# Top-k attention with two MLPs on one Trainium2 core: the hand-over to the first MLP block gets priority, score evictions go by whole tiles, rounding goes to GpSimd, and two weight rows start early

## The chip, the cores and the metric

The kernel runs on 1 core of one Trainium2 chip (trn2). The metric is device time in microseconds (us); the time before is the median of 3 runs. The engines are TensorE (PE in the profile, its weight loads PEld), VectorE (DVE), ScalarE (ACT), GpSimd (POOL) and SyncE (SP, which issues the loads and stores). Each engine works its own queue strictly in the order in which the program was built.

## The reference

Attention for 4 batches and 8 heads, 576 tokens, head dimension 64, in which each row of scores keeps its 32 largest; then two MLPs over the 2304 tokens of 512 values. q, k and v are float32; the weights reach the kernel as float64.

```python
scores = scale * np.matmul(q, k.transpose(0, 1, 3, 2))
kth = np.partition(scores, -top_k, axis=-1)[..., -top_k:-top_k + 1]
scores = np.where(scores >= kth, scores, -1000000000.0)
attn = np.exp(scores - np.max(scores, axis=-1, keepdims=True))
attn = attn / (np.sum(attn, axis=-1, keepdims=True) + 1e-09)
x = np.matmul(attn, v)                    # to (2304, 512)
h = np.maximum(x @ w_in, 0.0);   x = h * h @ w_out           # first MLP, d_ff 2048
h = x @ w_in2;   out = np.maximum(0.01 * h, h) @ w_out2      # second MLP
```

## The kernel before, in words

**High and low parts.** To keep float32 accuracy at the fast matmul format, most operands are split in two: a rounded high part and the low part left over (`xh`, `xl`; weights `wi`, `wo` hold both; so do `KT` and `q`). The high part is a rounding copy (`split_hi`, on ScalarE for the units in `HI_SET` and on GpSimd otherwise), the low part a subtraction, mostly on GpSimd. A product of two split operands takes three matmuls.

**Attention.** The tokens are cut into 9 units of 64 to 320 tokens (`UNITS`), each for 4 head pairs; these give 144 tiles of 128 rows, which are worked in 72 pairs. For a tile, TensorE makes scores in two halves of 288 columns (`scores`), ScalarE copies each half out of PSUM, VectorE finds the 32 largest by four MAX8 and three MATCH_REPLACE8 passes, ScalarE makes the exponentials (`drop`, `expo_sum`) with a shift `nb` from GpSimd (`shifts`), the sum's reciprocal `rc` takes a step on GpSimd and one on VectorE (`recip`), TensorE transposes (`pt_main`, `pt_left`) and multiplies with v (`av`), and `x_out` writes `xh` (ScalarE) and `xl` (GpSimd) for that head pair's 128 rows of x. Batches 2 and 3 (`EARLY`) have their scores made ahead of time: tiles `sp` in PSUM, copied into `stage` and stored to DRAM (`sd`), loaded again later. This filling runs over the slots `FILL`. Batch 0 uses PSUM tiles `sd`, batch 1 `att`. PSUM has 8 banks: 3 for `att`, and before the MLPs begin `SPB` for `sp` and `SDB` for `sd`.

**MLPs.** The tokens form 6 blocks (`BLOCKS`, the first of 512). A phase is one block and one MLP: 16 weight rows f, each with 12 matmuls into `h` (4 head pairs c, three products), the activation (ScalarE, GpSimd), and 12 matmuls that add into 4 `acc` banks. In the first two phases the weight rows are fresh: each is loaded (`wraw`), passed through two ScalarE passes and two VectorE steps (these make float32 out of the float64 words), rounded on ScalarE, subtracted on GpSimd, and stored (`wd`) for later phases.

**What sets the order.** Everything is put at slots; a slot is about one VectorE pass, 16 to a pair (`at`). A scheduling layer then makes each engine's queue out of this, by priorities: steps put at slots have a raised one, the MLPs' matmuls none. Block 0 needs units 0 and 1, that is pairs 0 to 15; it begins when `x_out` of pair 15's head pair has been put down.

Of the kernel before, what the change touches and what calls it, by code (L numbers as in the profile page):

```python
# [71 lines left out]
def topk_attention_moe_moe2_kernel(  # L72
# [117 lines left out]


# [361 lines left out]
    def moe(j, layer):  # L553
# [5 lines left out]
        gs = {}  # L559
        for f in range(NF + LAG):  # L560
            conv = iter(())
            if f < NF:
# [5 lines left out]
                h = late["psum"].tile([P, 512], F, tag="h", name="h", bufs=1)  # L568
                cnt = 0
                if f == 0:  # L570
                    mm = [(w, c, 0) for w in range(2) for c in range(NK)] + [(0, c, 1) for c in range(NK)]
                else:
                    mm = [(0, c, y) for c in range(NK) for y in range(2)] + [(1, c, 0) for c in range(NK)]
                for w, c, y in mm:
                    PE.matmul(h[:, 0:n], lhsT=wi[:, w, c * P:(c + 1) * P], rhs=x[c][y][:, 0:n], start=cnt == 0,  # L575
                              stop=cnt == 3 * NK - 1)
                    cnt += 1
                    if cnt % MQ == 0 and cnt < 3 * NK:
# [326 lines left out]
```

## Time and profile before

| | |
|---|---|
| median of 3 runs | 1211.68 us (1209.5 to 1212.38) |
| the profiled execution's own time | 1210.15 us |
| its span, first to last instruction | 1208.4 us, 20261 instructions |
| busy in the span | PE 94%, PEld 82%, DVE 78%, ACT 67%, POOL 57% |
| mean granted TensorE clock | 0.98 of full |

The shares are means over stages that differ: VectorE is nearly full until about 970 us and has little to do behind that, while the MLPs go on to the end on TensorE. The time of a run is a little longer than the span, by what lies ahead of the first and behind the last instruction.

### The profile page before, as it was taken

The numbers are of one execution on the slowest core, as the hardware profiler recorded it, in microseconds if no ns is written. First come the engines' busy times: TensorE is split into PE (matmuls) and PEld (weight loads), VectorE is DVE, ScalarE is ACT, GpSimd is POOL, SyncE is SP. The second block draws the span as 40 slices with busy tenths as digits, with TensorE's granted clock in tenths as the row PEclk, the third lists the DMA queues.
The fourth block names the chain that finished last, engine by engine and source line by source line (L and its number), as shares of the span: only waits on it lengthen the run. The fifth ranks groups of instructions, "written<-read, shape, count | busy, mean of one in ns | idle before, by whom it ended". The sixth has DMA issues, their size and how long they took to land.

```text
span 1208.4 us, 20261 instructions
## 1 busy us (share of the span) xinstructions
PE 1135.8 (94%) x6388; PEld 992.5 (82%) x6388; DVE 946.5 (78%) x1944; ACT 807.5 (67%) x1831; POOL 682.8 (57%) x982
## 2 busy tenths in 40 slices
PE   4988987999889999999999999999999999999998
PEld 3776765887678779988999898888788899999997
DVE  7999899868988999999999999999999930110122
ACT  6988898878998986766656666555666653334322
POOL 7765564877878876556666665555565644004300
PEclk9899897999999999999999999999999999999999
DMA  9765566779989888879988888776676679779974
GB/s 307 255 217 192 192 220 222 267 233 333 342 280 319 305 267 263 296 269 384 355 293 290 298 272 286 221 227 226 201 239 211 199 255 369 253 253 341 356 256 135
DMA packets 110522, 323.25 MB, mean 268 GB/s; under 512 B 17488, under 2 KB 25680, under 8 KB 110416
## 3 DMA queue, kind: packets, MB, share of 16 engines
q1 hardware_dynamic: 107776, 317.24, 77.5%
q10 hardware_dynamic: 2640, 4.72, 1.1%
q8 instruction: 52, 0.85, 0.3%
q14 instruction: 54, 0.44, 0.1%
HBM read 254.54 MB, written 67.37 MB: 266 GB/s over the span
## 4 chain that ended last, share of the span: by engine, by line
PE 71%; ACT 11%; DVE 7%; DMA 6%; issue 2%; POOL 1%; ACTq 0%; SPq 0%; POOLq 0%; DVEq 0%
PE h L575 29%; PE acc L620 14%; PE acc L618 14%; PE att L408 4%; PE att L313 4%; DVE m L829 3%; PE att L397 3%; DVE w L831 3%; DMA wraw<-in_w_dram 2%; DMA sd<-stage 2%; ACT stage L277 1%; ACT e L299 1%; ACT e L295 1%; ACT s L277 1%; PE sp L276 1%
## 5 line engine op out<-in xcount | busy, mean ns | idle before, releaser
L575 PE MATMUL h<-xh,wi 128*128 128x512 f32 (+2 forms) x1280 | 349.9, 345 | 13.4 <-ACT gb L597 4.2
L829 DVE MAX8 m<-w 128x8 f32<-128x576 f32 x432 | 311.9, 748 | 1.1
L575 PEld LDWEIGHTS h<-xh,wi 128*128 128x128 f32 x1280 | 227.5, 191 | 42.6 <-ACT gb L597 5.8
L831 DVE MATCH_REPLACE8 w<-m,w 128x576 f32<-128x576 f32 x288 | 213.5, 744 | 0.8
L575 PE MATMUL h<-xl,wi 128*128 128x512 f32 (+2 forms) x640 | 207.6, 342 | 0.6 <-DVE xl L632 0.6
L601 POOL TENSOR_TENSOR gl<-ga,gh 128x512 fp32r<-128x512 f32 (+2 forms) x160 | 162.7, 1017 | 37.9 <-ACT gh L600 32.1
L618 PE MATMUL acc<-gh,wo 128*128 128x512 f32 (+2 forms) x768 | 156.8, 340 | 0.0
L620 PE MATMUL acc<-wo,gh 128*128 128x512 f32 x576 | 152.5, 399 | 2.9 <-ACT gh L600 2.7
L598 POOL TENSOR_TENSOR ga<-ga,gb 128x512 f32<-128x512 f32 (+2 forms) x80 | 81.4, 1017 | 130.6 <-ACT gb L597 127.3
L618 PEld LDWEIGHTS acc<-gh,wo 128*128 128x128 f32 x768 | 126.5, 189 | 11.0 <-ACT gh L586 0.2
L575 PEld LDWEIGHTS h<-xl,wi 128*128 128x128 f32 x640 | 121.4, 191 | 12.3 <-DVE xl L632 1.1
L295 ACT ACTIVATE e<-s,m 128x576 f32<-128x576 f32 x144 | 111.7, 779 | 18.6 <-DVE m L829 13.4
L620 PEld LDWEIGHTS acc<-wo,gh 128*128 128x128 f32 x576 | 104.3, 189 | 24.1 <-ACT gh L600 5.0
L829 DVE MAX8 m<-s 128x8 f32<-128x576 f32 x144 | 104.1, 748 | 12.5 <-ACT s L277 6.1
L299 ACT ACTIVATE e<-e,nb 128x576 f32<-128x576 f32 x144 | 111.0, 774 | 3.2 <-POOL nb L289 2.8
L587 POOL TENSOR_TENSOR ga<-ga 128x512 f32<-128x512 f32 (+2 forms) x80 | 66.1, 827 | 78.1 <-ACT gh L586 72.8
L831 DVE MATCH_REPLACE8 w<-m,s 128x576 f32<-128x576 f32 x144 | 107.1, 744 | 0.6
L313 PE MATMUL att<-ident,e 128*128 128x128 f32 x576 | 90.8, 281 | 13.7 <-ACT e L299 5.1
L313 PEld LDWEIGHTS att<-ident,e 128*128 128x128 f32 x576 | 70.0, 143 | 27.4 <-ACT e L299 10.1
L308 POOL TENSOR_SCALAR e<-e,rc 128x576 f32<-128x576 f32 x108 | 79.8, 749 | 22.5 <-DVE rc L304 21.1
L585 ACT ACTIVATE ga<-h 128x512 f32<-128x512 f32 (+2 forms) x80 | 39.0, 488 | 77.4 <-PE h L575 71.9
L618 PE MATMUL acc<-gl,wo 128*128 128x512 f32 (+2 forms) x384 | 87.7, 345 | 0.1
(94 smaller groups left out, 2136.7 us busy)
## 6 DMA issues: line engine op xcount, KB each, us to landing
wi<-wd SPq DMA_DIRECT2D x160, 512.0 KB, 5.0
wo<-wd SPq DMA_DIRECT2D x160, 512.0 KB, 5.2
wraw<-in_w_dram SPq DMA_DIRECT2D x64, 512.0 KB, 6.0
sd<-stage SPq DMA_DIRECT2D x72, 288.0 KB, 2.9
s<-sd SPq DMA_DIRECT2D x72, 288.0 KB, 4.6
wd<-wi SPq DMA_DIRECT2D x32, 512.0 KB, 5.4
wd<-wo SPq DMA_DIRECT2D x32, 512.0 KB, 5.9
kraw<-in_k_dram SPq DMA_DIRECT2D x16, 576.0 KB, 5.4
```

The lines of the kernel that those rows point to most:

```text
L295: ACT.activation(t["e"], t["s"], AF.Prelu, bias=pr["m8"][:, i, 31:32], scale=-1.0, alpha=0.125 / FAR)
L299: ACT.activation(e, e, AF.Exp, bias=pr["nb"][:, i:i + 1], scale=-FAR, accum_out=pr["sum"][:, i:i + 1])
L308: POOL.tensor_scalar(e, e, pr["rc"][:, i:i + 1], 1.0, op0=OP.mult, op1=OP.mult)
L313: PE.transpose(ps[:, j * P:(j + 1) * P], t["e"][:, j * P:(j + 1) * P], ident)
L575: PE.matmul(h[:, 0:n], lhsT=wi[:, w, c * P:(c + 1) * P], rhs=x[c][y][:, 0:n], start=cnt == 0, stop=cnt == 3 * NK - 1)
L587: POOL.tensor_tensor(a[:, 0:n], a[:, 0:n], a[:, 0:n], op=OP.mult)
L598: POOL.tensor_tensor(a[:, 0:n], a[:, 0:n], b[:, 0:n], op=OP.subtract)
L601: (DVE if j >= GLD else POOL).tensor_tensor(gl[:, 0:n], a[:, 0:n], gh.bitcast(F)[:, 0:n], op=OP.subtract)
L618: PE.matmul(acc[c][:, 0:n], lhsT=wo[:, w, cs], rhs=g[:, 0:n], start=first, stop=last)
L620: PE.matmul(acc[c], lhsT=g[:, cs], rhs=wo[:, w, :], start=first, stop=last)
L829: cur["dve"] = DVE.max(out=m8[:, x, 8 * r:8 * r + 8], in_=t["s"] if r == 0 else t["w"])
L831: cur["dve"] = DVE.match_replace(out=t["w"], in_to_replace=m8[:, x, 8 * r:8 * r + 8], in_values=t["s"] if r == 0 else t["w"], imm_value=NEG)
```

## The change

- `scores`: for the batches made ahead, both halves go to one two-bank PSUM tile and are copied out by one 576-column copy. `SPB` is 2 of these (4 banks), `SDB` 1.
- `FILL` ends at slot 215 in place of 245.
- `HI_SET` is (0, 1): from the third head pair of unit 0 on, the rounding of q, k and v goes from ScalarE to GpSimd.
- Pair 15 (`first_done`): its steps from `shifts` to `x_out` are put right behind its last MAX8 and with a higher priority (`urgent`); its `av` goes in two halves by head, the first earlier.
- Weight rows 0 and 1: their ScalarE passes are made early (`lead_passes`, into PSUM banks of `sp`), their VectorE steps and the rounding, now on GpSimd, are put at pair 15's end (`lead_bits`).
- In the first phase, weight rows 0 and 1 have the 9 products of the first three head pairs issued ahead (`AHEAD`); the last head pair's three follow when it is there. Row 1 uses an `acc` bank for it. `ga` has 3 buffers.

```diff
@@ constants
-FILL = (2, 245)
+FILL = (2, 215)
-SDB = 2
-SPB = 3
+SDB = 1
+SPB = 2
+URGENT = 800
-HI_SET = (0, 1, 2, 3, 4, 5, 6, 7, 8, 9, 10, 11, 12, 13, 14, 15)
+HI_SET = (0, 1)
@@ scores
-            ps = stage_psum.tile([P, 512], F, tag="sp", name="sp", bufs=SPB)
+            if half == 0:
+                t["ps"] = stage_psum.tile([P, 2, 512], F, tag="sp", name="sp", bufs=SPB)
+            ps = t["ps"][:, half]
...
-        ACT.activation(t["s"][:, ks], ps[:, 0:HALF], AF.Copy)
+        if direct(uh):
+            ACT.activation(t["s"][:, ks], ps[:, 0:HALF], AF.Copy)
+        elif half == 1:
+            ACT.activation(t["s"].rearrange("p (x c) -> p x c", x=2), t.pop("ps")[:, :, 0:HALF], AF.Copy)
@@ new
+    def urgent(fn):
+        def run(*a):
+            with tc.high_priority(offset=URGENT):
+                fn(*a)
+        return run
...
+    def lead_passes(i):
+        led[i] = []
+        for raw, w in zip(wraw.pop(i), w_alloc(i)):
+            lo, hi = raw[:, :, 0], raw[:, :, 1]
+            b = pool.tile([P, 512], U, tag="wc", name="wc", bufs=WCB)
+            if not led[i]:
+                vs = stage_psum.tile([P, 2, 512], F, tag="sp", name="sp", bufs=SPB)
+            v = vs[:, len(led[i])]
+            ACT.activation(b, lo, AF.Copy, scale=L_SCALE, bias=L_BIAS)
+            ACT.activation(v, hi.bitcast(F), AF.Copy, scale=H_SCALE)
+            led[i].append((b, v.bitcast(U), w))
+
+    def lead_bits(i):
+        for b, vu, w in led.pop(i):
+            with behind("dve"):
+                DVE.scalar_tensor_tensor(b, vu, 3, b, op0=OP.logical_shift_left, op1=OP.bitwise_or)
+            DVE.scalar_tensor_tensor(b, vu, 0x80000000, b, op0=OP.bitwise_and, op1=OP.bitwise_or)
+            split_hi(w[:, 0, :], b.bitcast(F))
+            POOL.tensor_tensor(w[:, 1, :], b.bitcast(F), w.bitcast(F)[:, 0, :], op=OP.subtract)
@@ moe
+        ahead_of = AHEAD if j == 0 and layer == 0 else 0
+        for f in range(ahead_of):
+            hs[f] = late["psum"].tile([P, 512], F, tag="acc" if f else "h", name="h", bufs=4 if f else 1)
+            mm = [(w, c, y) for c in range(NK - 1) for w, y in ((0, 0), (1, 0), (0, 1))]
+            for i, (w, c, y) in enumerate(mm):
+                PE.matmul(hs[f][:, 0:n], lhsT=wt[base + f][0][:, w, c * P:(c + 1) * P], rhs=x[c][y][:, 0:n],
+                          start=i == 0, stop=False)
...
+                if f in hs:
+                    h = hs.pop(f)
+                    mm = [(w, NK - 1, y) for w, y in ((0, 0), (1, 0), (0, 1))]
...
-                a = late["mlp"].tile([P, 512], F, tag="ga", name="ga", bufs=2)
+                a = late["mlp"].tile([P, 512], F, tag="ga", name="ga", bufs=3)
@@ pairs and av
+        if p == first_done:
...
+            at(z + 13, urgent(shifts), pr)
+            for i in range(2):
+                at(z + 13, urgent(drop), pr, i)
+                at(z + 13, urgent(expo_sum), pr, i)
+            at(z + 13, urgent(recip), pr)
+            for i in range(2):
+                at(z + 14, urgent(pt_main), pr["t"][i])
+            at(z + 14, urgent(pt_left), pr)
+            continue
...
-        apart = uh["n"] > P and uh["n"] % P and uh["ti"] % 2 == 0
+        tight = uh["last"] // 2 == first_done
+        apart = uh["n"] > P and (uh["n"] % P or tight) and uh["ti"] % 2 == 0
...
+                at(z + i, urgent(av) if near else av, uh, hs, i)
+            at(z + nq, urgent(x_out) if near else x_out, uh, hs)
@@ weight rows 0 and 1
-    at(rslot[0] - 28, convert_now, 0)
-    at(rslot[0] - 14, convert_now, 1)
...
+    for i, z in enumerate((218, 232)):
+        at(z - 40, w_raw, i)
+        at(z, lead_passes, i)
+        at(16 * first_done + 13, lead_bits, i)
+        at(rslot[0] - 30 + i, w_raw, i + 2)
```

What this makes of the queues, at three places. The line numbers of the changed program are its own.

GpSimd from the second of pair 15's two `nb` steps to the low part of the last head pair, before. `m_2438` holds pair 16's maxima; `KT` and `q` are parts of batch 1, `wi` and `wo` the low parts of weight rows 0 and 1:

```order
L289 TENSOR_SCALAR nb<-nb 128x2
L521 TENSOR_TENSOR wi<-wc,wi 128x512
L238 TENSOR_TENSOR KT<-kraw,KT 64x576 x2
L521 TENSOR_TENSOR wo<-wc,wo 128x512
L303 TENSOR_SCALAR sum<-sum 128x2
L288 TENSOR_TENSOR nb<-m_2438 128x2
L521 TENSOR_TENSOR wi<-wc,wi 128x512
L289 TENSOR_SCALAR nb<-nb 128x2
L255 TENSOR_TENSOR q_78<-qraw,q_77 128x256
L521 TENSOR_TENSOR wo<-wc,wo 128x512
L303 TENSOR_SCALAR sum<-sum 128x2
L432 TENSOR_TENSOR xl_653<-xn,xh_652 128x256
```

The same stretch after the change begins with `nb` of pair 15, whose maxima are `m_2205`; TENSOR_SCALAR of `q` and `KT` are the roundings that ScalarE made before:

```order
L300 TENSOR_TENSOR nb<-m_2205 128x2
L116 TENSOR_SCALAR q_83<-qraw 128x256
L116 TENSOR_SCALAR KT<-kraw 128x576 x2
L262 TENSOR_TENSOR q_84<-qraw,q_83 128x256
L301 TENSOR_SCALAR nb<-nb 128x2
L444 TENSOR_TENSOR xl_647<-xn,xh_646 64x256
L262 TENSOR_TENSOR q_84<-qraw,q_83 128x256
L245 TENSOR_TENSOR KT<-kraw,KT 64x576 x2
L116 TENSOR_SCALAR wi<-wc 128x512 x2
```

After two more rows (the sum's step and a rounding of `wo`) it goes on to the low part of the last half head pair. `m_2351` is pair 16:

```order
L556 TENSOR_TENSOR wi<-wc,wi 128x512
L116 TENSOR_SCALAR wo<-wc 128x512
L556 TENSOR_TENSOR wi<-wc,wi 128x512
L556 TENSOR_TENSOR wo<-wc,wo 128x512
L116 TENSOR_SCALAR KT<-kraw 128x576 x2
L556 TENSOR_TENSOR wo<-wc,wo 128x512
L245 TENSOR_TENSOR KT<-kraw,KT 64x576
L300 TENSOR_TENSOR nb<-m_2351 128x2
L245 TENSOR_TENSOR KT<-kraw,KT 64x576
L444 TENSOR_TENSOR xl_647<-xn,xh_646 64x256
```

The part between the two steps of `nb`, one row before, now holds a rounding of q, one of K and a q subtraction, and between `nb` and the last `xl` stand the roundings of K and of both weight rows as well as their low parts.

TensorE at the hand-over, before: transposes of pair 16 (`e_107`, `e_108`) between weight row 0's twelve products and row 1's first ones.

```order
L313 MATMUL att<-ident,e_107 128x128 x4
L575 MATMUL h<-xh_652,wi 128x512 x5
L575 MATMUL h<-xl_653,wi 128x512 x4
L313 MATMUL att<-ident,e_108 128x128 x4
L575 MATMUL h<-xh_652,wi 128x512
L575 MATMUL h<-xl_653,wi 128x512
L575 MATMUL h<-xh_652,wi 128x512
L575 MATMUL h<-xl_653,wi 128x512
L575 MATMUL h<-xh_652,wi 128x512
```

After: pair 15's last transposes and the second half of its `av`, then the 18 products that don't need the last head pair (L601), among them the two `rc` transposes of pair 15, and the remaining ones of both rows (L621):

```order
L338 MATMUL att<-ident,e_110 64x128
L325 MATMUL att<-ident,e_110 128x128 x2
L409 MATMUL att<-PT,VN 128x256 x5
L601 MATMUL h<-xh_646,wi 128x512 x2
L359 MATMUL att<-ident,rc 128x128 x2
L601 MATMUL h<-xh_646,wi 128x512
L601 MATMUL h<-xl_647,wi 128x512
L601 MATMUL h<-xh_646,wi 128x512 x2
L601 MATMUL h<-xl_647,wi 128x512
L601 MATMUL h<-xh_646,wi 128x512 x2
L601 MATMUL h<-xl_647,wi 128x512
```

...and some rows on, the first products with the last head pair, `xh` of both rows, one half of scores, then `xl` of both:

```order
L601 MATMUL h<-xh_646,wi 128x512 x2
L601 MATMUL h<-xl_647,wi 128x512
L621 MATMUL h<-xh_646,wi 128x512 x4
L285 MATMUL att<-KT,q_77 128x288
L285 MATMUL att<-KT,q_78 128x288
L621 MATMUL h<-xl_647,wi 128x512 x2
```

Pair 16's transposes have moved behind weight row 4's products, and the products of rows 0 and 1 lie ahead of them and of any product into `acc`.

VectorE ahead of pair 15's last MAX8, which is the last row of each piece; before:

```order
L304 RECIPROCAL rc<-sum 128x2
L428 TENSOR_TENSOR xn<-att,rb 128x256
L829 MAX m_2312<-w 128x8 x2
L514 SCALAR_TENSOR_TENSOR wc<-att,wc 128x512
L831 MATCH_REPLACE w<-m_2312,w 128x576
L831 MATCH_REPLACE w<-m_2438,s_103 128x576
L515 SCALAR_TENSOR_TENSOR wc<-att,wc 128x512
L514 SCALAR_TENSOR_TENSOR wc<-att,wc 128x512
L829 MAX m_2312<-w 128x8
```

After:

```order
L316 RECIPROCAL rc<-sum 128x2
L440 TENSOR_TENSOR xn<-att,rb 128x256
L898 MATCH_REPLACE w<-m_2205,w 128x576
L896 MAX m_2351<-s_104 128x8
L898 MATCH_REPLACE w<-m_2351,s_103 128x576
L896 MAX m_2205<-w 128x8
L896 MAX m_2351<-w 128x8
L898 MATCH_REPLACE w<-m_2205,w 128x576
L898 MATCH_REPLACE w<-m_2351,w 128x576
L896 MAX m_2205<-w 128x8
```

The three SCALAR_TENSOR_TENSOR steps of weight row 0 have moved behind pair 15, and two more passes of pair 16 (`m_2351`) stand ahead of its end.

## Rows read from the trace of the kernel before

**Rows 1.** Table of stretches: busy us (instructions) by engine, granted clock, DMA.

```profile
0.00:180.00 180.00, 144.16 (x798) 117.05 (x798) 165.38 (x354) 155.26 (x418) 119.32 (x213) 0.96 0.71 230
180.00:207.00 27.00, 18.99 (x66) 12.87 (x66) 26.04 (x55) 22.52 (x50) 10.51 (x15) 0.68 0.68 233
207.00:400.00 193.00, 181.59 (x876) 147.77 (x877) 160.48 (x303) 168.02 (x347) 155.49 (x165) 0.98 0.85 293
400.00:1000.00 600.00, 588.41 (x3451) 523.62 (x3450) 564.40 (x1179) 391.93 (x863) 363.05 (x542) 0.99 0.80 268
1000.00:1208.00 208.00, 202.69 (x1202) 191.18 (x1200) 30.20 (x56) 69.72 (x157) 34.48 (x48) 0.99 0.80 281
```

**Rows 2.** Timeline of VectorE, around pair 15's end: start, length, engine, line.

```profile
175.69 0.69 DVE L514 SCALAR_TENSOR_TENSOR wc<-att,wc 128x512 uint32<-128x512 uint32 x1 [0.25 <-ACT att L510]
...
178.94 1.41 DVE L829 MAX8 m<-w 128x8 f32<-128x576 f32 x2
...
201.68 0.42 DVE L428 TENSOR_TENSOR xn<-att,rb 128x256 f32<-128x256 f32 x1
```

**Rows 3.** Timeline of GpSimd, the same stretch.

```profile
179.77 0.20 POOL L288 TENSOR_TENSOR nb<-m 128x2 f32<-128x2 f32 x1 [0.42 <-DVE m L829]
...
203.71 0.74 POOL L432 TENSOR_TENSOR xl<-xn,xh 128x256 fp32r<-128x256 f32 x1 [6.00 <-ACT xh L429]
```

**Rows 4.** Timeline of TensorE, one earlier av group and the hand-over.

```profile
98.99 2.52 PE L397 MATMUL att<-PT,VN 128*128 128x256 f32 x10
...
193.79 6.67 PE L397 MATMUL att<-PT,VN 128*128 128x256 f32 x18
...
202.15 0.66 PE L313 MATMUL att<-ident,e 128*128 128x128 f32 x4
203.68 1.43 PE L575 MATMUL h<-xh,wi 128*128 128x512 f32 x5 [0.87 <-ACT xh L429]
...
209.28 1.07 PE L575 MATMUL h<-xh,wi 128*128 128x512 f32 x4
210.18 2.03 PE L618 MATMUL acc<-gh,wo 128*128 128x512 f32 x8
```

**Rows 5.** Groups by form on GpSimd, whole span: count, busy us, mean ns, idle.

```profile
L521 POOL TENSOR_TENSOR wo<-wc,wo 128x512 fp32r<-128x512 f32 x32 | 41.5, 1295 | 5.5 <-ACT wo L519 5.2
...
L587 POOL TENSOR_TENSOR ga<-ga 128x512 f32<-128x512 f32 x32 | 33.3, 1040 | 26.0 <-ACT gh L586 25.8
...
L238 POOL TENSOR_TENSOR KTa<-kraw,KTa 64x576 fp32r<-64x576 f32 x16 | 22.4, 1414 | 0.7
...
L115 POOL TENSOR_SCALAR q<-qraw 128x320 fp32r<-128x320 f32 x24 | 11.0, 458 | 24.5 <-PE sp L276 22.6 <-PE att L276 1.9
L115 POOL TENSOR_SCALAR KTa<-kraw 128x576 fp32r<-128x576 f32 x16 | 10.4, 670 | 1.9 <-DMA kraw<-in_k_dram 1.9
...
L115 POOL TENSOR_SCALAR q<-qraw 128x256 fp32r<-128x256 f32 x16 | 6.4, 404 | 11.0 <-PE sp L276 6.8 <-DMA qraw<-in_q_dram 4.0
L432 POOL TENSOR_TENSOR xl<-xn,xh 128x256 fp32r<-128x256 f32 x8 | 5.9, 734 | 6.6 <-ACT xh L429 6.5
```

**Rows 6.** Groups by form on ScalarE, 0 to 400 us.

```profile
L277 ACT ACTIVATE stage<-sp 128x288 f32<-128x288 f32 x144 | 53.1, 437 | 13.0 <-DMA sd<-stage 5.4 <-PE sp L276 5.2 <-issue 2.0
...
L113 ACT ACTIVATE KT<-kraw 128x576 fp32r<-128x576 f32 x16 | 10.2, 699 | 2.8 <-DMA kraw<-in_k_dram 2.8
...
L113 ACT ACTIVATE q<-qraw 128x256 fp32r<-128x256 f32 x24 | 9.8, 431 | 3.0 <-DMA qraw<-in_q_dram 2.4 <-PE att L276 0.4
```

**Rows 7.** Waits of TensorE, 207 to 400 us: total us, times, longest.

```profile
PE h L575 <- ACT wi L519: 3.1, 2, 1.6
```

**Rows 8.** Waits of VectorE to 210 us, of GpSimd to 180 us.

```profile
DVE m L829 <- ACT e L295: 5.6, 4, 2.8
...
POOL q L115 <- PE sp L276: 29.4, 14, 4.1
```

**Rows 9.** Chain that ended last, 170 to 190 us: start, us, what.

```profile
176.78 5.87 DMA kraw<-in_k_dram
```

More of the change, by code (lines that the diff above doesn't have):

```diff
@@ L500, in w_convert_steps @@
     def w_convert_steps(i):
-        if i >= len(steps) or not fresh[i]:
+        if i >= len(steps) or not fresh[i] or i in wt:
             return
@@ L542, in topk_attention_moe_moe2_kernel @@
     MQ = 3
+    AHEAD = 2
     def rows(g0, n):
@@ L567, in moe @@
                 wi, wo = wt.pop(si)
[L568 to L571, printed above, removed]
-                else:
[L573 to L578, printed above, removed]
+                if f in hs:
+                    h = hs.pop(f)
+                    mm = [(w, NK - 1, y) for w, y in ((0, 0), (1, 0), (0, 1))]
+                else:
+                    h = late["psum"].tile([P, 512], F, tag="h", name="h", bufs=1)
+                    if f == 0:
+                        mm = [(w, c, 0) for w in range(2) for c in range(NK)] + [(0, c, 1) for c in range(NK)]
+                    else:
+                        mm = [(0, c, y) for c in range(NK) for y in range(2)] + [(1, c, 0) for c in range(NK)]
+                for cnt, (w, c, y) in enumerate(mm):
+                    PE.matmul(h[:, 0:n], lhsT=wi[:, w, c * P:(c + 1) * P], rhs=x[c][y][:, 0:n],
+                              start=cnt == 0 and f >= ahead_of, stop=cnt == len(mm) - 1)
+                    if cnt % MQ == MQ - 1 and cnt < len(mm) - 1:
                         next(conv, None)
@@ L605, in moe @@
                 yield
-            if f >= LAG:
-                ff = f - LAG
+            if f < ahead_of - 1:
+                for _ in conv:
+                    pass
+                w_raw(si + 4)
+                continue
+            for ff in range(0 if f == ahead_of - 1 else f - LAG, f - LAG + 1):
+                if ff < 0:
+                    continue
                 if ff == 0:
@@ L734, in topk_attention_moe_moe2_kernel @@
     pairs = []
+    first_done = next(uh["last"] // 2 for uh in uhs if uh["hp"] == NHP - 1 and uh["u"]["g0"] + uh["n"] >= BLOCKS[0])
     for p in range(NPAIRS):
@@ L738, in topk_attention_moe_moe2_kernel @@
         z = 16 * p
+        if p == first_done:
+            assert all(direct(t["uh"]) and not split(t["uh"]) for t in pr["t"])
+            for i, t in enumerate(pr["t"]):
+                at(z - DLEAD + 5 * i, scores, t, 0)
+                at(z - DLEAD + 2 + 5 * i, scores, t, 1)
+            at(z + 13, urgent(shifts), pr)
[6 more added lines that the diff above has]
+            at(z + 14, urgent(pt_left), pr)
+            continue
         for i, t in enumerate(pr["t"]):
@@ L771, in topk_attention_moe_moe2_kernel @@
             continue
-        apart = uh["n"] > P and uh["n"] % P and uh["ti"] % 2 == 0
+        tight = uh["last"] // 2 == first_done
+        apart = uh["n"] > P and (uh["n"] % P or tight) and uh["ti"] % 2 == 0
         for hs in ((0,), (1,)) if apart else ((0, 1),):
-            z = 16 * (uh["lastA"] // 2 if hs == (0,) else uh["last"] // 2) + 30
+            near = tight and hs[-1] == 1
+            z = 16 * (uh["lastA"] // 2 if hs == (0,) else uh["last"] // 2) + (15 if near else 27 if tight and apart else 30)
             nq = 2 * len(hs)
             for i in range(nq):
-                at(z + i, av, uh, hs, i)
-            at(z + nq, x_out, uh, hs)
+                at(z + i, urgent(av) if near else av, uh, hs, i)
+            at(z + nq, urgent(x_out) if near else x_out, uh, hs)
         z += nq
```

8 lines of the change are left out of this document (3 added, 5 removed).

## The prediction

> **What bounds the kernel now.** I read the table of stretches first, since an average over the span hides the stages. In [rows 1] TensorE is busy 588.4 of the 600 us between 400 and 1000, and 202.7 of the last 208: from 400 us on some 17 us of idle TensorE are left in all, so what is to be gained must come from earlier. VectorE (the top-k passes) is busy 564 of those 600 us, so there two engines are nearly full, and a lead of one alone would be lost. The stretch from 180 to 207 us is the odd one: TensorE is busy 19.0 of 27 us at a granted clock of 0.68, ScalarE 22.5, GpSimd 10.5. That is the hand-over from attention to the first block's multiplications.
>
> The timelines show what fills it. Pair 15 is the last that block 0 needs. Its last MAX8 is the first of the two at 178.94 [rows 2]; nb on GpSimd, which waits for it, starts at 179.77 [rows 3]. I call the end of that MAX8 T: 179.7. After it come drop, exp, the sum, the transposes, the av products (18 in one row from 193.79, in 6.67 us [rows 4]), xn on VectorE at 201.68 [rows 2] and the low part xl, which ends at 203.71 + 0.74 = 204.45 [rows 3]. From T to xl it takes 24.8 us; the reader should see that the steps themselves are short, and that most of it is queueing behind other pairs' steps. Weight row 0's products start at 203.68, and row 1's are done when the next group starts, at 210.18 [rows 4]. From 207 to 400 us TensorE is busy 181.6 of 193 us [rows 1]; the longest of its waits there is for ScalarE's weight rounding [rows 7].
>
> **The change, part by part.**
>
> *T itself.* VectorE's queue loses three SCALAR_TENSOR_TENSOR steps ahead of T (the one at 175.69 is the first), 0.69 us each, and gets two more top-k steps of pair 16 there, 0.70 each [rows 2]: T becomes 179.0. Other things can move it. ScalarE loses before T some ten K roundings at 0.70 and two dozen of q at 0.43 or less, 16 us [rows 6]. 144 half evictions at 0.44 become 72 whole ones; a 576-column copy out of PSUM isn't in the trace, the nearest is the K rounding at 0.70 [rows 6], so each saves 0.17 and all of them 12 us, less where halves ran back to back; I take 6, with 0 and 12 as ends. VectorE waited 5.6 us for ScalarE's drops before 210 us [rows 8]; without these T comes 5 us earlier. Against it, GpSimd takes the roundings (K 0.67, q 0.40 [rows 5]), about 15 us, in a queue that runs in order and already stands still 29.4 us there until TensorE frees q buffers [rows 8]. The new work fits into such waits where it lies right, and delays scores where not; and the direct scores now have one PSUM bank in place of two. I let these cancel, with 5 us either way.
>
> *Rounding by GpSimd after T.* This term decides. In the new order GpSimd has, from nb of pair 15 to the last xl: four K highs at 0.67 and four K lows at 1.41 (8.3 us), one q high at 0.40 and two q lows at 0.73 (1.9), four weight lows at 1.29 (5.2), four weight highs, two xl at 0.73 (1.5) and four small steps at 0.2 (0.8), all by [rows 3, 5]. A 512-column rounding isn't in GpSimd's trace; between 0.46 for 320 and 0.67 for 576 columns lies 0.61, so 2.4 us. Sum 20.0 us. Ahead of nb the queue is late by about 2.5 us: between pair 14's sum and this nb stand a K split (4.2), an xl (0.7), three q highs (1.2), two q lows (1.5) and four short q steps (0.8), 8.4 us, while the two pairs' ends lie some 9.5 us apart, of which pair 14's nb, exponentials and sum take the first 2.6; a K load inside adds the rest. The raw K buffer is single: a load goes out when the K low steps are done and lands 5.87 us later [rows 9], then the next K high can go. At one of its two places in this stretch that costs 1.9 us. So xl ends at T + 2.5 + 20.0 + 1.9 = T + 24.4 = 203.4, against 204.45. **The prioritised steps bring xl hardly earlier: GpSimd's queue takes back what the other queues give.** Ends: T + 21.5 without the late queue and the load, T + 30 if a K load is late by its own length again.
>
> *Early products.* Eighteen of the 24 products of weight rows 0 and 1 need only the first three head pairs. They need the low weights too, 14.9 and 16.8 us after T by the same count, and take 18 x 0.225 = 4.1 us at the pace of [rows 4] (four from 209.28 to 210.18). Four more need the last xh, about T + 19 on ScalarE, where it stands behind weight passes whose buffers GpSimd frees. When xl comes, two products are left, 0.5 us: both rows are done at 203.9, before at 210.18, so 6.3 us. Before, pair 16's eight transposes lie within that time, 0.66 us for four [rows 4]; in the new order they come later: 1.3 less. **Lead 5.0 us.** Since the work of rows 0 and 1 is the same, the early products gain only in that they fill a time in which TensorE waits for GpSimd; with that cover gone they gain nothing.
>
> The clock bears on this. In 180 to 207 us the granted clock was 0.68 of full [rows 1], a mixture of the two levels 1.2 and 2.4 GHz; the 18 av products took 0.37 us each, where ten at 98.99 took 0.25 [rows 4]; from 207 to 400 it was 0.98. TensorE was idle much of the time before, and the new order leaves it as idle. The Trainium skill ("TensorE: Matmul & The Clock Gate", What's actually happening) says that an idle engine is held at half clock and that activity releases it; the trace agrees (0.68, then 0.98). By full clock the sum stands; by half clock the early products take 8.1 us and the last six 2.7, and the lead is 4.2.
>
> *What follows.* Each weight row then needs 24 products, 5.4 us of TensorE. GpSimd has for it two weight lows and gl at 1.29 and a square at 1.04 [rows 5], 4.9 us, so it stays just under TensorE. From 207 to 400 us it gets 7 us more (q and v) on 155.5 of 193, and ScalarE loses 7 of 168 [rows 1]. ScalarE's relief could take part of TensorE's 11.4 us of waits there, GpSimd's load could add as much; I count nothing. VectorE is busy 160.5 of these 193 us [rows 1], so attention has room to come 5 us earlier too, and from 400 us on I let the lead stand. The third ga buffer only frees waits of ScalarE that TensorE doesn't see.
>
> Merged evictions have a rule against them: the Trainium skill ("Perfetto Trace Analysis", Optimizing Scalar/DVE Operations) says that where an engine isn't saturated but causes bubbles elsewhere, smaller instructions may let work end sooner. ScalarE was busy 155 of the first 180 us [rows 1], and no run here shows merged ones. By it T comes later, as in the rival of a late queue.
>
> **Sum.** 1210.15 (the profiled execution: span 1208.4 and 1.75 around it) - 5.0 is 1205.15. The median of the runs shown, 1211.68, is 1.5 above it, so 1206.7.
>
> **Rivals.**
> - *The lead is given back by 400 us.* ScalarE at 168 of 193 us and GpSimd at 155 + 7 feed the 32 fresh weight rows; if they set the pace and not TensorE, an earlier start only lets TensorE wait longer. For it: TensorE's longest wait there names ScalarE [rows 7]. Against it: all its waits there are 11.4 of 193 us. Time 1210 to 1213. Chance 0.25.
> - *GpSimd comes late, and the kernel is slower.* More K, q and weight work stands ahead of the last xl and of the direct scores. It decides once xl ends after 208.4 (5.0 beyond 203.4), and beyond that each us costs one; one K load late by its length and T late by 5 us give 1206.7 + 10.9 = 1217.6. For it: the 29.4 us that the queue stands still. Against it: it is busy 119 of the first 180 us. Chance 0.19.
> - *More is gained.* T comes 5 us earlier, or half of TensorE's 11.4 us of waits goes: 1196 to 1202. Chance 0.12.
> - My forecast, 1203 to 1209: 0.44.
>
> **Numbers.** A measurement of this kernel tells some 0.3%, 3.6 us, from no change. Faster takes the larger gain and nearly all of the forecast (0.12 + 0.41), same the given-back lead and a little of the rest, slower the late queue. The range reaches from 1197, most of the larger gain, to 1217, most of the late queue.
>
> **What would show it.** In the profile after: T between 174 and 184; the last xl on GpSimd 22 to 27 us behind it, with GpSimd almost without gaps between; 18 products before it, and both weight rows done some 5 us earlier; TensorE's idle time from 207 to 400 us about the same. It is wrong if xl comes soon after T (a short queue: then 10 us or more are gained), if T has moved by over 5 us, or if TensorE's idle time between 207 and 400 grows by what was gained.

## The result, and the profile after

The change made the kernel slower: 1222.12 us, median of 4 runs (1220.6 to 1223.47), against 1210.59 of the kernel before in the same session. The ratio is 1.0093, with a 95% interval of 1.0075 to 1.0111. The profiled execution after has a span of 1218.5 us, 10.1 more than before.

The table of stretches of the kernel after (busy us with instructions in brackets, for TensorE, its weight loads, VectorE, ScalarE and GpSimd, then granted clock, DMA share, GB/s) answers to [rows 1]:

```profile
0.00:180.00 180.00, 142.84 (x750) 113.68 (x750) 155.71 (x325) 137.93 (x301) 115.30 (x219) 0.93 0.69 232
180.00:207.00 27.00, 19.95 (x87) 14.15 (x86) 27.00 (x58) 14.20 (x30) 23.95 (x39) 0.81 0.39 120
207.00:400.00 193.00, 182.55 (x883) 147.50 (x882) 166.18 (x316) 170.01 (x350) 166.09 (x187) 0.99 0.88 304
400.00:1000.00 600.00, 584.88 (x3388) 518.54 (x3388) 570.60 (x1194) 392.25 (x863) 361.01 (x538) 0.99 0.79 263
```

ScalarE got its relief (137.9 busy us to 180, before 155.3), and yet VectorE, the engine that makes T, does 325 instructions there in place of 354. The next fence is the timeline of VectorE around pair 15's end:

```profile
189.53 1.40 DVE L896 MAX8 m<-w 128x8 f32<-128x576 f32 x2
...
192.30 0.74 DVE L896 MAX8 m<-w 128x8 f32<-128x576 f32 x1
192.97 1.26 DVE L553 SCALAR_TENSOR_TENSOR wc<-sp,wc 128x512 uint32<-128x512 uint32 x2
194.16 0.40 DVE L440 TENSOR_TENSOR xn<-att,rb 64x256 f32<-64x256 f32 x1
```

T, the end of pair 15's last MAX8, is 192.30 + 0.74 = 193.0; before it was 179.7 [rows 2]. The timeline of GpSimd from there on, beside [rows 3]:

```profile
194.77 0.20 POOL L300 TENSOR_TENSOR nb<-m 128x2 f32<-128x2 f32 x1
...
203.03 0.19 POOL L315 TENSOR_SCALAR sum<-sum 128x2 f32<-128x2 f32 x1
...
214.02 0.72 POOL L444 TENSOR_TENSOR xl<-xn,xh 64x256 fp32r<-64x256 f32 x1
```

The last xl ends at 214.74, so T + 21.7, and GpSimd has almost no gap between. TensorE there, beside [rows 4]:

```profile
206.07 0.73 PE L601 MATMUL h<-xh,wi 128*128 128x512 f32 x2
...
210.83 1.07 PE L621 MATMUL h<-xh,wi 128*128 128x512 f32 x4
211.74 0.43 PE L285 MATMUL att<-KT,q 128*128 128x288 f32 x2
214.80 0.73 PE L621 MATMUL h<-xl,wi 128*128 128x512 f32 x2 [2.64 <-POOL xl L444]
```

The early products (L601) run from 206.07, the four with the last xh follow, and behind xl only two products are left. Both weight rows are done at 215.53, 0.8 us behind xl, but 5.3 later than before. What VectorE waited for up to 195 us says where T went (total us, times, longest); TensorE's and ScalarE's waits follow:

```profile
DVE m L896 <- ACT s L287: 12.9, 11, 2.3
...
PE sd L285 <- ACT s L287: 11.8, 24, 1.1
PE sp L285 <- ACT stage L289: 10.1, 13, 1.9
...
ACT s L287 <- PE sd L285: 12.3, 15, 1.0
ACT stage L289 <- PE sp L285: 10.6, 7, 3.4
...
POOL q L116 <- PE sp L285: 18.6, 10, 3.1
POOL q L116 <- PE sd L285: 16.9, 7, 6.6
```

Two of these in the kernel before, over the same stretch:

```profile
DVE m L829 <- ACT s L277: 1.3, 1, 1.3
...
PE sd L276 <- ACT s L277: 0.6, 2, 0.3
```

VectorE's waits for s went from 1.3 us, once, to 12.9. TensorE waits 24 times for ScalarE to empty the single sd bank (the PSUM tile of batch 0's scores), ScalarE 15 times for TensorE to fill it: the two take turns. Three halves of batch 0's scores on TensorE, from its timeline, show one such turn, 1.3 us for products that take 0.78 (ScalarE's copy of a half took 0.41):

```profile
190.47 0.78 PE L285 MATMUL sd<-KT,q 128*128 128x288 f32 x4
191.83 0.76 PE L285 MATMUL sd<-KT,q 128*128 128x288 f32 x4 [0.59 <-ACT s L287]
193.09 0.80 PE L285 MATMUL sd<-KT,q 128*128 128x288 f32 x4 [0.50 <-ACT s L287]
```

And the last wait, GpSimd's rounding of q for 16.9 us behind TensorE's sd products, is new: the roundings stand in GpSimd's queue until the buffer is free, and what is behind them stands too.

### The profile page after: what moved, and what is told of

Same layout as the page of the kernel before. It is cut to its first block, busy times and chain, and to the rows that moved or that the text cites. A ratio compares the mean times of both kernels' runs of the same rounds, so it can differ in the third digit from the quotient of the medians.

```text
span 1218.5 us, 20130 instructions
## 1 busy us (share of the span) xinstructions
PE 1143.0 (94%) x6388; PEld 995.3 (82%) x6388; DVE 950.1 (78%) x1945; ACT 787.4 (65%) x1708; POOL 705.8 (58%) x1035
## 4 chain that ended last, share of the span: by engine, by line
PE 56%; DVE 5%; ACT 1%; issue 0%; POOL 0%; DVEq 0%; ACTq 0%
PE h L621 24%; PE acc L669 12%; PE acc L671 12%; PE att L420 4%; PE att L325 3%; DVE m L896 2%; DVE w L898 2%; PE att L285 1%; PE att L338 1%; DVE PTs L331 0%; DVE xl L683 0%; ACT e L307 0%; ACT e L311 0%; ACT PTs L330 0%; DVE PTs L348 0%
## 5 line engine op out<-in xcount | busy, mean ns | idle before, releaser
L621 PE MATMUL h<-xh,wi 128*128 128x512 f32 (+2 forms) x1268 | 346.4, 345 | 5.1 <-ACT xh L682 2.3
L621 PEld LDWEIGHTS h<-xh,wi 128*128 128x128 f32 x1268 | 224.9, 190 | 31.1 <-ACT xh L682 4.3
L621 PE MATMUL h<-xl,wi 128*128 128x512 f32 (+2 forms) x634 | 206.2, 343 | 4.1 <-POOL xl L444 2.6
L621 PEld LDWEIGHTS h<-xl,wi 128*128 128x128 f32 x634 | 120.4, 191 | 16.9 <-DVE xl L683 3.4
L645 ACT ACTIVATE gh<-ga 128x384 fp32r<-128x384 f32 (+2 forms) x112 | 58.6, 523 | 50.0 <-POOL ga L643 40.0
```

## The experiments

Every kernel was compared with the kernel before on its own chip. From the profiled execution of each I read five marks, from the timelines: **nb15**, the start of pair 15's nb on GpSimd (at T or up to 2.5 us behind it); **row 8, 88, 96**, the start of the step that writes gh, the rounded activation, on ScalarE for that weight row, counted from 0 through the kernel (32 rows for each block; row 96 is block 3's first); **p51**, the start of pair 51's nb (the last pair that block 3 needs). Times in us.

| kernel | ratio to before (95%) | nb15 | row 8 | row 88 | p51 | row 96 | span |
|---|---|---|---|---|---|---|---|
| before | 1 | 179.8 | 264.6 | 708.6 | 731.6 | 754.1 | 1208.4 |
| after | 1.0093 (1.0075–1.0111) | 194.8 | 268.6 | 712.4 | 739.3 | 763.5 | 1218.5 |
| e1_halves | 1.0103 (1.0071–1.0135) | 183.1 | 257.1 | 713.8 | 742.6 | 770.3 | 1225.6 |
| e4_round_act | 1.0054 (1.0036–1.0073) | 185.2 | 260.3 | 710.7 | 732.8 | 757.9 | 1210.4 |
| e7_halves_act | 1.0035 (1.0015–1.0055) | 179.8 | 251.6 | 705.1 | 725.0 | 753.1 | 1207.1 |
| e2_merged_alone | 1.0195 (1.0163–1.0226) | 195.8 | 281.9 | 719.6 | 745.5 | 771.4 | 1225.5 |
| e3_one_sd_alone | 1.0184 (1.0168–1.0201) | 191.2 | 273.4 | 719.9 | 746.1 | 774.5 | 1231.3 |
| e11_pool_alone | 1.0024 (1.0000–1.0049) | 180.1 | 260.3 | 705.4 | 727.3 | 753.8 | 1209.3 |
| e12_fill215_alone | 0.9995 (0.9977–1.0013) | 179.4 | 266.5 | 710.4 | 733.4 | 755.8 | 1212.0 |
| e9_handover_alone | 1.0108 (1.0092–1.0123) | 179.8 | 258.2 | 712.4 | 734.8 | 762.9 | 1218.4 |
| e6_no_early | 1.0095 (1.0079–1.0110) | 193.3 | 268.9 | 720.0 | 742.5 | 765.9 | 1219.1 |
| e17_no_early_healthy | 1.0088 (1.0066–1.0110) | 180.3 | 256.9 | 705.5 | 735.0 | 762.4 | 1220.1 |
| e19_rows_later | 1.0084 (1.0063–1.0106) | 180.4 | 264.7 | 700.0 | 729.7 | 757.9 | 1214.5 |
| e20_rows_later_merged | 1.0189 (1.0155–1.0223) | 185.2 | 267.9 | 712.4 | 742.3 | 770.1 | 1226.6 |
| e14_less_vector | 0.9997 (0.9985–1.0009) | 179.3 | 264.0 | 709.6 | 721.3 | 753.8 | 1206.3 |
| e15_less_tensor | 0.9963 (0.9948–0.9979) | 179.1 | 264.9 | 694.6 | 726.9 | 748.2 | 1200.6 |
| e16_less_both | 0.9945 (0.9927–0.9962) | 178.8 | 263.3 | 697.9 | 720.3 | 744.4 | 1198.2 |
| e21_less_vector_after | 0.9976 (0.9961–0.9991) | 179.2 | 255.6 | 707.1 | 719.4 | 748.4 | 1205.8 |
| e22_edge_steps | 1.0008 (0.9991–1.0024) | 179.5 | 251.2 | 707.9 | 727.8 | 754.3 | 1205.9 |
| e24_edge_fill200 | 0.9995 (0.9980–1.0011) | 179.9 | 252.9 | 707.1 | 727.0 | 753.5 | 1205.1 |

One profiled execution can lie some us from the median of its kernel (those of e1, e2 and e12 lie 6 to 8 us off), so verdicts on time go by the ratio, those on place by the marks.

### The banks of the scores

**e1_halves**, the staged scores by halves again:

```diff
-SDB = 1
-SPB = 2
+SDB = 2
+SPB = 3
...
-            if half == 0:
-                t["ps"] = stage_psum.tile([P, 2, 512], F, tag="sp", name="sp", bufs=SPB)
-            ps = t["ps"][:, half]
+            ps = stage_psum.tile([P, 512], F, tag="sp", name="sp", bufs=SPB)
...
+        ACT.activation(t["s"][:, ks], ps[:, 0:HALF], AF.Copy)
```

> The changed kernel with the staged scores evicted half by half again (three single sp banks and two sd banks), all else as changed. Theory A (one bank for the direct scores makes VectorE wait for ScalarE's s, 12.9 us against 1.3, so T comes at 193 and not at 180): VectorE's waits for s go back to about 1 to 3 us before T, T comes at 178 to 184, the last xl 20 to 24 us behind it, time 1205 to 1212. Rival B (GpSimd's in-order queue with the K and q roundings holds the direct scores back): T stays at 189 to 194, time 1217 to 1222. Rival C (the shorter fill, 215, crowds ScalarE and TensorE before T): the same as B.

T came back, nb15 at 183.1, and VectorE's waits for s to 1.5 us; the time did not, 1.0103. Theory A was right on T and wrong on the time.

**e2_merged_alone** is the kernel before with the opposite edit, **e3_one_sd_alone** the kernel before with only the numbers changed:

```diff
-SDB = 2
-SPB = 3
+SDB = 1
+SPB = 4
```

> The kernel before with the merged evictions alone (two double sp banks, one sd bank). Theory A: T at 187 to 194 and time 1217 to 1225, since VectorE waits some 10 us for s. Rivals B and C: T within 3 us of 179.7, time 1205 to 1213.

> The kernel before with one sd bank in place of two and four single sp banks in place of three; evictions by halves, all else as before. Theory A, if the number of banks of the direct scores is what counts: T at 185 to 192, time 1215 to 1222. If it is the merged eviction itself (a longer ScalarE step, and a staged tile that waits for both its halves) T stays within 3 us of 179.7 and the time within 1208 to 1213.

Both cost nearly the same, 1.0195 and 1.0184, with nb15 at 195.8 and 191.2. In e3 the evictions are the halves of before, so it is the second bank that is missed, not the halves. VectorE's waits up to 195 us in e2, and to 190 us VectorE's and TensorE's in e3:

```profile
DVE m L834 <- ACT s L280: 10.5, 12, 2.1
```

```profile
DVE m L829 <- ACT s L277: 5.6, 7, 2.1
...
PE sd L276 <- ACT s L277: 12.4, 22, 1.2
```

TensorE's wait for the sd bank is there in e3 too, 12.4 us in 22 waits.

### The roundings

**e4_round_act** is the changed kernel with the roundings on ScalarE again, **e7_halves_act** that with e1's edit too; **e11_pool_alone** is the kernel before with the change's line:

```diff
-HI_SET = (0, 1)
+HI_SET = (0, 1, 2, 3, 4, 5, 6, 7, 8, 9, 10, 11, 12, 13, 14, 15)
```

> The changed kernel with the K and q roundings of all head pairs on ScalarE again, merged evictions kept. Theory A: VectorE still waits 10 us or more for s, T at 188 to 194, time 1214 to 1223. Rival B: T at 178 to 184, time 1204 to 1212. Rival C: T at 188 to 194.

> The changed kernel with evictions by halves and the roundings on ScalarE; fill up to 215, the hand-over and the early products kept. With one sd bank the direct scores were late (T at 185.1 with the roundings on ScalarE); with two T should be at 178 to 182. Theory H: what counts is pair 51; T 3 to 5 us earlier alone gives at most that, 1210 to 1216. If the fill up to 215 is what costs, T stays after 183 and the time above 1214.

> The kernel before with the K and q roundings on GpSimd alone. In the changed kernel these cost 7 to 9 us with the merged evictions and with halves alike (1222.1 against 1214.7, 1221.7 against 1212.2). Theory R (GpSimd's queue, in order, makes scores and weight lows late): T later by 2 to 8 us, time 1214 to 1222. If it only costs beside the hand-over's own weight work: T at 178 to 182, time 1206 to 1212.

With the after these make a square. On GpSimd: 1.0103 with halves and 1.0093 merged; on ScalarE: 1.0035 and 1.0054. So beside the hand-over the roundings on GpSimd cost 0.4 to 0.7%, 5 to 8 us, and the merged evictions with their single bank nothing that the intervals tell (0.2% one way, 0.1% the other). On nb15 both act: against e7's nb15 of 179.8 the roundings alone cost 3.4 us, the evictions alone 5.4, the two together 15.0. In the kernel before the roundings on GpSimd leave T where it was (180.1) and cost 0 to 0.5%. Expectation H for e7 held, and A's time for e4 (1214 to 1223); e4's T of 185 lay between A's and B's.

### The hand-over

**e9_handover_alone** is e7 with the fill up to 245; **e12_fill215_alone** the kernel before with 215:

```diff
-FILL = (2, 215)
+FILL = (2, 245)
```

> The changed kernel with evictions by halves, all roundings on ScalarE and the fill up to 245, as before: only the prioritised last steps, the lead weights' passes and the early products remain of the change. Theory V: T at 177 to 183, VectorE's waits for s below 3 us before T; both first weight rows done 4 to 8 us before 210.18, but pair 71 at 967 to 974, so time 1206 to 1213. Rival P: the lead of 5 us stands, 1202 to 1206. Rival D (the hand-over itself costs: the prioritised steps push back what feeds VectorE): pair 71 at 976 or later, time 1215 to 1222.

> The kernel before with the staged scores ending at slot 215 and not 245, alone. With the hand-over the fill up to 215 was worth 9 us (1212.2 against 1221.3), since what is still to be staged then no longer stands beside pair 15's last steps. Alone: T within 3 us of 179.7, time 1204 to 1211, faster if the same holds without the hand-over; 1211 to 1216 if the denser fill only crowds ScalarE before T.

In e9 T is where it was, the last xl ends 11.2 us earlier (193.2), and row 8 comes 6.4 us earlier: the hand-over does what it is written to do. The kernel is 1.08% slower: attention's pair 21 comes at 303.2 (before 286.8). Time and marks came as rival D had them, but that pair 21's lateness is what costs isn't shown: in e7 it is nearly as late (299.5), and pair 51 comes 6.6 us earlier than before. With the fill up to 215 (e7) nine us of the loss are gone; alone (e12) that edit does nothing. Why the fill's end matters beside the hand-over I didn't settle.

**e6_no_early** takes the early products out of the changed kernel, **e17_no_early_healthy** out of e7:

```diff
-    AHEAD = 2
+    AHEAD = 0
```

> The changed kernel without the early products alone (no products of weight rows 0 and 1 ahead of the last head pair; the rest as changed). Theory V: the first acc group starts 3 to 6 us later, at 224 to 227, but the pairs of attention don't move, and the time stays within 3 us of 1222. Rival P: 4 to 6 us slower, 1226 to 1228.

> The changed kernel with evictions by halves and roundings on ScalarE (1212.2 us, T as before), without the early products. They should then be worth their 3 to 6 us at weight row 8 (251.6 with them), so row 8 at 254 to 258. Theory H: at block 3's border that lead is cut, row 96 at 752 to 757 and time within 3 us of 1212. Rival P: 1215 to 1218.

In the changed kernel they are worth nothing (1.0095 against 1.0093, and row 8 comes only 0.3 us later without them, row 88 7.6). In e7, where T isn't late, they are worth 0.5%: 1.0088 without, 1.0035 with. H's price for e17 was wrong (1220.7 measured), and P's 1215 to 1218 nearer. But not by P's way: without them row 8 is 5.3 us later and row 88 only 0.4, while pair 51 is 10 us later.

**e19_rows_later** is e9, **e20_rows_later_merged** e4, with block 0's rows entered later:

```diff
...
+        if slot == rslot[0] + HOLD:
+            active.extend(moe(*ph) for ph in groups[0])
+            credit = 0.0
+            cur["rate"] = sum(quanta(*ph) for ph in groups[0]) / (rslot[1] - slot - 1)
...
+HOLD = 17
```

> The hand-over alone (evictions by halves, roundings on ScalarE, fill up to 245), but block 0's weight rows entered into the order of the program 17 slots later, where they stand in the kernel before, at the pace of before; the last steps stay prioritised. Theory H with rival D (block 0's rows, put ahead of the steps of pairs 16 to 21, make attention late: pair 21 was 16 us later, pair 51 3 us): pair 21 at 285 to 295, pair 51 at 729 to 733, row 96 at 752 to 756, time 1206 to 1212. If instead the prioritised steps themselves cost it: pair 21 stays after 298 and the time at 1216 to 1222.

> The changed kernel with the roundings on ScalarE (1214.7 us) and block 0's rows entered 17 slots later as well. Theory H with D: pairs 26 and 51 some 3 to 5 us earlier than without, time 1207 to 1213, the same as before or slightly faster. Else 1213 to 1220.

The marks of e19 came as D said (pair 21 at 289.5, pair 51 at 729.7), row 88 even 8.5 us earlier than before; the time did not (1.0084), and e20 was a plain miss (1.0189). In e19 the lead turns at row 96, 3.8 us later than before; its profiled span is 6.1 longer.

### The border of block 3

Row 96 stands 452 to 458 us ahead of the end in all twenty traces, though it comes anywhere from 744 to 775. So a us at row 96 is a us at the end, to within these 6 us. It needs all rows before it and the xl of pair 51, behind whose start it came by 3 to 8 us in each trace. Around it, the tables of stretches of the kernel before, the kernel after and e19 (columns as above):

```profile
745.00:750.00 5.00, 4.28 (x27) 3.43 (x26) 4.89 (x13) 2.94 (x8) 1.66 (x3) 1.00 0.76 245
750.00:755.00 5.00, 3.71 (x18) 2.55 (x17) 4.90 (x10) 3.54 (x7) 0.91 (x2) 1.00 0.96 333
```

```profile
745.00:750.00 5.00, 5.00 (x31) 4.54 (x31) 4.93 (x12) 2.69 (x7) 3.01 (x4) 1.00 0.81 258
750.00:755.00 5.00, 4.11 (x23) 3.29 (x21) 5.00 (x11) 4.81 (x11) 1.55 (x4) 1.00 0.85 245
755.00:760.00 5.00, 2.73 (x13) 2.01 (x14) 4.88 (x11) 2.12 (x5) 2.20 (x3) 0.87 0.97 333
760.00:765.00 5.00, 4.31 (x15) 3.13 (x14) 4.91 (x12) 2.41 (x6) 0.21 (x2) 0.79 0.50 153
```

```profile
740.00:745.00 5.00, 2.71 (x14) 1.67 (x12) 4.93 (x12) 3.59 (x8) 0.39 (x2) 1.00 0.81 270
745.00:750.00 5.00, 1.04 (x5) 1.04 (x6) 4.92 (x11) 2.50 (x7) 2.03 (x4) 0.53 0.88 285
750.00:755.00 5.00, 3.79 (x16) 2.82 (x14) 4.97 (x12) 1.26 (x2) 0.71 (x3) 0.79 0.16 51
755.00:760.00 5.00, 2.10 (x7) 1.75 (x8) 4.97 (x10) 4.25 (x10) 1.34 (x3) 0.89 0.47 164
```

VectorE (third busy column) stays full; TensorE (first) has nothing to do, 10.4 of 20 us in e19, and its clock falls. TensorE's timeline in e19 says for what:

```profile
748.96 1.12 PE L321 MATMUL att<-ident,e 128*128 128x128 f32 x4 [4.69 <-POOL e L316]
749.73 2.48 PE L615 MATMUL h<-xh,wi 128*128 128x512 f32 x5
...
757.90 0.50 PE L615 MATMUL h<-xh,wi 128*128 128x512 f32 x1 [4.11 <-ACT ga L624]
```

It waits for the attention of pair 51 (e, normalised by GpSimd), starts row 96, and waits for ScalarE. ScalarE's timeline shows that second wait, from a later pair's exponential to row 96's activation:

```profile
754.33 0.78 ACT L303 ACTIVATE e<-s,m 128x576 f32<-128x576 f32 x1 [3.62 <-DVE m L890]
...
757.27 0.58 ACT L624 ACTIVATE ga<-h 128x512 f32<-128x512 f32 x1
757.88 0.63 ACT L625 ACTIVATE gh<-ga 128x512 fp32r<-128x512 f32 x1
```

So e19's lead, still 7.4 us at row 95, goes in two steps: xl of pair 51 starts only 1.5 us earlier than before (749.60 against 751.12), and row 96's activation then stands in ScalarE's queue behind an exponential that waits 3.6 us for VectorE's maxima. It came 8.3 us behind that xl, where it came 3.0 behind it in the kernel before. In e17 and e20 the same order of ScalarE's queue stands there, and row 96 comes 8.3 and 8.2 behind xl.

Two cuts test what counts at the border. **e14_less_vector** is the kernel before with the first of these edits, **e15_less_tensor** with the second, **e16_less_both** with both, **e21_less_vector_after** e7 with the first:

```diff
-            elif i < 14:
+            elif i < 14 and not (r == 2 and 26 <= p < 36):
```

```diff
+                if j == 1:
+                    mm = [m for m in mm if m[0] == 0]
```

> The kernel before, with the third MATCH_REPLACE left out in ten pairs (26 to 35, at 409 to 540 us): 20 x 0.70 = 14 us less of VectorE, and the top 32 of these pairs are then not the true ones. Theory V (from some 500 us on VectorE, busy 98 of each 100 us, sets when a pair of attention ends and so the end: pair 71 at 970 plus some 238 us in every run so far): span 8 to 14 us shorter, time 1196 to 1203. Rival P (TensorE, busy 97 to 99 of each 100 us there, sets it, as the prediction took it): time within 3 us of 1210.

> The kernel before, with the products of the low input weights left out for block 1 in both layers (2 x 16 x 4 = 128 multiplications of 256 columns, some 17 us of TensorE at 452 to 582 us by 19.8 us for 128 of the same size; block 1's outputs then lack that part). Theory V: weight rows 40 to 63 come 10 us or more earlier, but pair 71 stays at 967 to 972 and the time within 3 us of 1210. Rival P: 10 to 17 us faster, 1193 to 1200.

> The kernel before with both cuts together: the third MATCH_REPLACE left out in pairs 26 to 35 (14 us of VectorE) and the low input weights' products left out in block 1 (some 17 us of TensorE); outputs differ by that. Theory H (weight row 96, block 3's first, needs attention's pair 51 and all rows before it; the end comes 452 to 457 us after it in every run): each cut alone moved row 96 only as far as the other engine let it (0.3 and 5.9 us); together row 96 comes 10 to 15 us earlier and the time is 10 to 15 us shorter, 1194 to 1199, more than the two alone together (0.6 and 6). Rival P (TensorE's work alone sets the end): as the TensorE cut alone, 1201 to 1205.

> The changed kernel with evictions by halves and roundings on ScalarE, with the third MATCH_REPLACE left out in pairs 26 to 35 (14 us of VectorE; outputs differ by that). In the kernel before this cut gained 0.6 us, since there TensorE was as late as attention at block 3's border. Here the weight rows come 2 to 10 us earlier there. Theory H: pair 51 at 714 to 718, row 96 at 744 to 749, time 1203 to 1208, a gain of 4 to 9 us on 1212.2. Rival P: within 2 us of 1212.

Theory V fell: 14 us less of VectorE in the kernel before bring pair 51 10.2 us earlier and the end nothing (0.9997), since there TensorE's rows are as late. Seventeen us less of TensorE give 4.5 (0.9963): row 88 gains 14.0, row 96 only 5.9. Both together give 0.9945, row 96 9.7 us earlier; H's mark nearly came, its time didn't (P's 1201 to 1205 did), so the two cuts add up, as far as the intervals tell, and no more. But on e7, where the rows lead, the VectorE cut that was worth nothing gives 0.6% (0.9976 against 1.0035, H's 4 to 9 us), and row 96 4.7 us. So the worth of that cut hangs on which engine is late at the border. The pair e15 and e16 supports this less: the rows lead there too, and the same cut gives 3.9 us at row 96 but a time inside the intervals (0.9963, 0.9945).

**e22_edge_steps** treats pair 51 as the change treats pair 15; **e24_edge_fill200** adds a shorter fill:

```diff
+        if p == EDGE:
...
+            at(z + 13, urgent(shifts), pr)
...
+EDGE = 51
```

> The changed kernel with evictions by halves and roundings on ScalarE (1212.2 us), and the last steps of pair 51, on which block 3's first weight row waits, also entered at slots 13 to 16 behind its pair and prioritised, as the change does for pair 15. Theory H (the lead of block 0's rows is cut where block 3 waits for pair 51, with TensorE idle some 4 us at 745 to 755): row 96 at 747 to 751, time 1205 to 1210. If the end doesn't hang on that border: within 3 us of 1212.

> The kernel with halves, roundings on ScalarE and pair 51's steps moved up (1.0008 of before), with the staged scores ending at slot 200 in place of 215. If less staging beside pair 15's hand-over is what made 215 better than 245 (9 us), the last part of it gives up to 3 us more: 1205 to 1210; if the denser staging only crowds ScalarE before T: T later than 181 and 1212 to 1217.

Pair 51's xl did not come earlier (749.86 against e7's 747.70), nor row 96. The ratios, 1.0008 and 0.9995, tell neither from the kernel before. No version here beats it.

## Why the prediction was wrong

The forecast was 5.0 us gained; by the ratio 11 were lost. With the merged evictions and single bank undone and the K and q roundings on ScalarE again (e7), 7 of these 11 come back (1.0093 to 1.0035); no gain is left even so. Two steps failed: the edits that were let cancel ahead of T, and the lead that was let stand behind it.

**T itself: the first step that failed.** Edits for and against were let cancel, 179.0 with 5 us either way; T was 193.0. The saving on ScalarE was sized about right (a merged copy took 0.65 us, 46.3 us for 72, so 0.22 saved on each, forecast 0.17), and the gain set against it did come: VectorE's waits for ScalarE's e fell from 5.6 us to 0.4 up to 195 us. But that was not the whole of what T hung on. The one PSUM bank, named in half a sentence and given no price, made VectorE wait 11.6 us more for s. The price could have been worked out: each direct half then runs product, eviction, product in turn. The Trainium skill ("Perfetto Trace Analysis", Matmuls) says that independent groups should rotate through different banks, so that the eviction of one overlaps the next; the trace agrees, with 24 waits of 0.5 us where before none of that size stood. The rule that the prediction did cite, on breaking up instructions, pointed at the same delay for another reason, and e3, slow with evictions by halves, shows that it wasn't that one. The roundings on GpSimd add 3.4 us to nb15 and, with the single bank, 9.6. But a late T alone isn't shown to be what costs: e1 has T back, its last xl ends at 202.59 and row 8 comes 7.5 us earlier than before, and it is as slow as the kernel after (1.0103). Of the 7 us that e7 takes back, most goes with the roundings (5 to 8 us) and the bank's part is not clear of zero.

**After T: right.** xl came at T + 21.7, at the low end that was worked out (T + 21.5, forecast T + 24.4). From nb to the end of xl it took 20.0 us, the sum of GpSimd's work in the forecast; nb was 1.7 us late (forecast 2.5), and no K load was waited for (forecast 1.9). A 512-column rounding took 0.62 us, estimated 0.61. So GpSimd's queue does set xl in the changed kernel. How much of that is the K and q roundings isn't settled: from nb to xl it is 17.2 us in e7 and 19.5 with the roundings (e1), but with the single bank 21.0 without them (e4) and 20.0 with them.

**Early products: right in place.** The 18 products stood ahead of xl, 0.23 us each, so at full clock, and the rows were done 0.8 us behind it (forecast 0.5). The lead of 5.0 that was to come of it is 5.3 us at row 8 in e7 (against e17), and 0.3 in the changed kernel (against e6).

**What follows: the second step that failed, hidden by T.** "From 400 us on I let the lead stand" fails between row 72 and block 3's border. In e7, where T is as before, the lead is 13.0 us at row 8, still 10.3 at row 72, 3.5 at row 88, 1.0 at row 96: the end is no better. From row 72 to row 96 (611.4 to 753.1 us) TensorE is busy 134.4 of 141.7 us in e7, in the kernel before 129.6 of 132.4 (621.7 to 754.1): of the 9.3 us lost, 4.5 are idle time more, and 4.8 work more. This fits attention's smaller lead (4.8 us at pair 41), by which more of its work still stood ahead of row 96. In e19 the lead holds up to row 95 and goes at the border. In the changed kernel itself TensorE had made up its lateness by row 72 (622.0, before 621.7), but attention had not: pair 41 was 8.0 us late and pair 51 7.7, VectorE being busy 98 us of each 100 from 500 us on. Row 96, which needs pair 51, came 9.4 us late, and the end 10.1. The table of stretches read as two nearly full engines was right; that a lead of one alone would be lost was said, and then not priced at the place where one has to wait for the other.

**The rivals.** "GpSimd comes late, and the kernel is slower" named the sign and the deciding point: xl ended at 214.74, past 208.4. By its rate of one for one, 6.3 us beyond the point, it gives 1218; T was late by 13 and not by 5. That xl decides is not borne out: in e1 it ended 5.8 us ahead of that point, and the time was the same. So the rival's sign came true, and its way was not shown. "The lead is given back" holds once T is repaired, but between 620 and 755 us, 200 us and more later than was thought.

**Open.** Why one sd bank costs 1.8 to 2.0% in the kernel before and nothing measurable beside the hand-over with fill 215 (e4 against e7); why e1, early at row 8, is 10 us late at row 32; why the early products move pair 51 by 10 us in e7; and why the scheduling layer puts a waiting exponential ahead of row 96's activation in some versions. The third ga buffer, the early ScalarE passes of weight rows 0 and 1 and their rounding on GpSimd were never taken out by themselves. Each edit let the whole order of the queues come out anew, and no experiment held that order fixed.

## What to carry to other kernels

Before merging evictions, count the buffers that the merged tile takes away from the neighbour that feeds the bounding engine: from two banks to one, product and eviction take turns, and that turn can be priced from the durations in the trace. Where two engines are both nearly full, look for the points where one must wait for the other, and price a lead there: in the runs here it was worth only about what the later of the two allowed. An expected gain that is shown at the edited place (here e7's rows 13 us earlier) should be followed along several marks to the end before it is counted.

## What was unexpected of the hardware

TensorE's clock fell in the middle of a stretch that is full on average. In e19 TensorE had nothing to do from 744.3 to 749.0 us, ahead of row 96, and the granted clock was 0.53 of full at 745 to 750, mostly the lower of its two levels of 1.2 and 2.4 GHz. Row 96's first five products then came 0.46 us apart (2.28 us from the first to the next group). After the second idle stretch, 4.1 us, the clock fell again, to 0.50 from 758.9 to 762.3, and the next row's products of 512 columns came 0.42 us apart (below), against 0.23 from 766 us on at full clock. In the kernel after it was 0.79 at 760 to 765, behind 2.3 idle us in the 5 before; in the kernel before it stayed at 1.00 from 735 to 765, where TensorE was idle 2.0 us in all.

```profile
758.93 0.63 PE L615 MATMUL h<-xh,wi 128*128 128x512 f32 x1
759.35 0.63 PE L615 MATMUL h<-xl,wi 128*128 128x512 f32 x1
759.78 0.63 PE L615 MATMUL h<-xh,wi 128*128 128x512 f32 x1
```
